# Weights converted in PSUM, squares mostly on GpSimd, raw weights in tiles of their own, half of batch 1's k^T q ahead of the FFN

## The chip, the cores and the metric

The kernel runs on one core of one Trainium2 chip. Its metric is the time of one execution on the device in microseconds (us), the median of several. Five engines work from instruction streams of their own: TensorE (PE), VectorE (DVE), ScalarE (ACT), GpSimd (POOL) and SyncE (SP), which here issues every DMA.

## The reference

Channel attention is followed by a feed-forward layer with a rational activation. B = 4, N = 6080, C = 256, d_ff = 2048. q, k, v are fp32, the two weight matrices fp64.

```python
qn = q / (norm(q, axis=1) + 1e-6);  kn = k / (norm(k, axis=1) + 1e-6)
a = softmax(kn.transpose(0, 2, 1) @ qn / tau)         # [B, 256, 256]
x = (v @ a).reshape(B * N, 256)
h = x @ w_in                                          # [24320, 2048]
g = (a0 + a1 h + a2 h^2 + a3 h^3) / (1 + |b0||h| + |b1| h^2 + 1e-6)
out = g @ w_out
```

## The kernel before

Each batch has 12 groups of 512 rows (the last has 448), 48 groups in all. The work is written as steps, each with an engine, an estimated cost, a key (a due time), the buffers it reads and writes, and a mark for steps that use the ports shared by VectorE and GpSimd. `Planner.order` plays these steps through before the kernel is built: on every engine it takes the ready step with the lowest key whose buffers are free, and writes down the order. On the chip each engine runs its steps in exactly that order. `SLOTS` says how many buffers a tag has; for the tags of the `fifo` list they are given out strictly in the order of the keys of the steps that open them.

**Attention (`Attn`).** A batch is read in 24 halves of a group, k and q of 256 rows, 512 KB (two DMAs). For a half ScalarE squares both (`ACT`, into an `sq` buffer), and the squares are added to one running sum: for batch 0 by VectorE, for the others by GpSimd. TensorE adds the products k^T q: batch 0 in one PSUM slot `hx` over all 24 halves, the other batches per pair of halves in an `hx` slot, which VectorE adds to `sacc` in SBUF. `softmax` then folds the sum, makes the norms, scales the scores into an `sq` buffer (`sn`), takes exponentials into a second one (`ex`), transposes, and `fuse` multiplies the attention into w_in for eight column blocks p (`w` buffers, split into a high and a low part).

**Weights (`piece`).** The fp64 weights come as pairs of 32-bit words, in 16 pieces of 512 KB: eight of w_in, eight of w_out. For each, ScalarE takes one absolute value and VectorE six operations of 512 elements make an fp32 piece. The first four pieces (`early`) use the tags `d`, `uu`, `r`; the other twelve have the raw words in `kq`, and work in `cv` and `cv2`. All of this is in SBUF.

**Main loop.** For each of the 48 groups `values` transposes v and splits it. `pair` does two blocks of 128 columns of the hidden layer, eight pairs a group, 384 in all: 12 matmuls into an `hx` slot, some twelve elementwise operations on ScalarE, VectorE and GpSimd, and 8 products with w_out (16 records) into the PSUM slot `acc`; `finish` copies `acc` out. PSUM holds three `hx` slots and one `acc`, each of two banks. Pairs p in `FACTORED` (p = 1 and 7, from the second group on) get the denominator from a VectorE product in place of GpSimd's addition. `LAG` holds the due times of a pair's steps behind its first, `TIME` those of all else; `T0` = 48.71 is the key of the first pair. Batch 1's attention has keys from T0 on, so it runs beside the first groups.

Of the kernel before, what the change touches and what calls it, by code (L numbers as in the profile page):

```python
# [18 lines left out]


LAG = {
    "first": 2.89, "prod": 5.51, "abs": -9.36, "line": 9.43, "second": 4.09, "sum": -23.2, "slope": 4.25,
    "num1": 24.9, "num2": 15.62, "root": 7.62, "one": 1.56, "square": 8.72, "again": 13.14, "quot": 7.51,
    "last": 10.86, "out": 34.22,
}
TIME = {
    "pair": 3.65, "start": 48.71, "load": 1.9, "softmax": 55.08, "in": 7.55, "late_in": 4.93, "out0": 1.91,
    "out": 6.15, "attn0_0": -0.12, "attn_0": 0.95, "attn0": 3.78, "attn": 2.7, "attn1": 91.81, "value": 3.3,
    "fuse": 1.89, "finish": 9.56,
}  # L30


# [35 lines left out]
class Planner:  # L68
# [1 line left out]

    HOP = {"PE": 0.25, "ACT": 0.07, "DVE": 0.07, "POOL": 0.07, "SP": 2.0}

    def __init__(self, slots, fifo, banks):
        self.slots, self.fifo, self.banks = slots, fifo, banks
# [34 lines left out]
    def order(self):  # L111
# [10 lines left out]
        events, out, now = [], [], 0.0  # L122
        port = {"DVE": 0.0, "POOL": 0.0}
        for s in self.steps:
            if not s.need:
# [13 lines left out]
        while left:  # L139
            for e in ready:  # L140
                while busy[e] <= now and ready[e]:
                    skipped, pick = [], None
                    while ready[e]:
                        entry = heapq.heappop(ready[e])
                        if fits(entry[2]):
                            pick = entry[2]
                            break
                        skipped.append(entry)
                    for entry in skipped:
                        heapq.heappush(ready[e], entry)  # L150
                    if pick is None:
                        break
                    for b in pick.new:
                        b.slot = free[b.tag].pop(0)
                        if b.tag in queue:
                            queue[b.tag].pop()
                    out.append((now, pick))
                    left -= 1
                    busy[e] = now + pick.cost
                    if pick.port:  # L160
                        other = "POOL" if e == "DVE" else "DVE"
                        busy[e] = max(now, port[other]) + pick.cost
                        port[e] = busy[e]
                    for b in pick.banks:
                        b.owner, b.until = e, busy[e] + self.HOP[e]
                    heapq.heappush(events, (busy[e], 0, pick.n, pick))
                    heapq.heappush(events, (busy[e] + self.HOP[e], 1, pick.n, pick))
            if not left:
                break
            assert events, [(e, h[0][0], [b.tag for b in h[0][2].new], dict(free)) for e, h in ready.items() if h]  # L170
            now = events[0][0]
            while events and events[0][0] <= now:
                _, what, _, s = heapq.heappop(events)
                for t in s.after:
# [14 lines left out]
def tile_channel_attention_rational_ffn(  # L189
# [15 lines left out]
    P = 128  # L205
# [9 lines left out]
    while n0 < N:  # L215
# [5 lines left out]
    TG = B * NG  # L221


    FACTORED = (1, 7)

    pe = InOrder(tc, nc.tensor)
    dve = InOrder(tc, nc.vector)
# [2 lines left out]
    sp = InOrder(tc, nc.sync)  # L230

    SLOTS = {"hx": 3, "acc": 1, "d": 4, "uu": 4, "r": 3, "g": 4, "w": 10, "kq": 4, "sq": 2, "ssq": 1,
             "vst": 1, "vhi": 2, "vlo": 2, "orow": 2, "sacc": 1, "eT": 1, "cv": 2, "cv2": 1, "n2": 1,
             "s0": 1, "y": 1, "e": 1, "sm": 1}
    plan = Planner(SLOTS, ("d", "uu", "r", "g", "w", "kq", "sq", "cv", "cv2", "vst", "vhi", "vlo", "orow"), ("hx", "acc"))
# [59 lines left out]
    def piece(side, m, at, c):  # L295
# [5 lines left out]
            src = w_in[j * P : (j + 1) * P, cols]  # L301
        else:
            src = w_out.rearrange("(f p) e -> p f e", p=P)[:, 2 * m : 2 * m + 2, :]
        early = side == "in" and m < 4
        raw = buf("d" if early else "kq", [P, 2 * PIECE], U32, "raw")
        work = buf("uu" if early else "cv", [P, 2, PIECE], F32, "work")
        unit = buf("r" if early else "cv2", [P, PIECE], U32, "unit")

        def keep():
            return work[:, 0]  # L310

        def top(kind=U32):
            return work[:, 1].bitcast(kind)

        def load():
# [4 lines left out]
        def lo():  # L320
            return raw.tile.rearrange("p (n w) -> p n w", w=2)[:, :, 0]
# [9 lines left out]
            dve.scalar_tensor_tensor(top(), hi(), 0xC0000000, top(), op0=ALU.bitwise_and, op1=ALU.bitwise_or)  # L331

        def power():
            dve.tensor_scalar(unit.tile, top(), 0xFF800000, None, op0=ALU.bitwise_and)

        def low_word():

            rest = unit.tile.bitcast(F32)
            dve.scalar_tensor_tensor(rest, lo(), 2.0**-52, rest, op0=ALU.mult, op1=ALU.mult)

        def together():
            rest = unit.tile.bitcast(F32)
            dve.tensor_tensor(rest, rest, top(F32), op=ALU.add)

        def cut_off():


            dve.scalar_tensor_tensor(
                dst, keep(), 1.125 * 2.0**-15, unit.tile.bitcast(F32), op0=ALU.is_ge, op1=ALU.mult
            )  # L350

        if side == "in":
            dst, ok = w_in_sb[:, j, cols], w_in_ok[part, j]
        else:
            dst, ok = w_out_sb[:, 2 * m : 2 * m + 2].rearrange("p f e -> p (f e)"), w_out_ok[m]
        step("SP", 1.5, at, load, (), [raw])
        step("ACT", 0.67, c, lambda: act.activation(keep(), hi().bitcast(F32), AF.Abs), [raw], [work])
        step("DVE", 0.45, c, low_bits, [raw, work], [work], True)
        step("DVE", 0.7, c + 0.1, high_bits, [raw, work], [work], True)
        step("DVE", 0.45, c + 0.2, power, [work], [unit], True)  # L360
        step("DVE", 0.7, c + 0.3, low_word, [raw, unit], [unit], True)
        step("DVE", 0.7, c + 0.4, together, [work, unit], [unit], True)
        step("DVE", 0.7, c + 0.5, cut_off, [work, unit], [ok], True)


    class Attn:
# [3 lines left out]
        def __init__(self, b, begin, pace, end, gate=()):  # L370
            self.b, self.gate, self.kq = b, gate, [None, None]
            self.ssq = None
            first = b == 0
            sps = buf("hx", [P, 2, GT], F32, "sps") if first else None
            self.sacc = None if first else buf("sacc", [P, 512], F32)
            for i in range(2 * NG):
                both = begin + (i if first else i + 1 - i % 2) * pace
                self.half(i, begin + i * pace, both, sps)
            self.scores = sps if first else self.sacc
            self.softmax(end)  # L380

        def half(self, i, at, both, sps):
# [2 lines left out]
            g, half = divmod(i, 2)  # L385
            base, pn = groups[g]
            first = self.b == 0
            kq = buf("kq" if not first or i % 6 < 3 else "r", [P, T // 2, 2, C], F32, "kq")

            def load():  # L390
                for j, src in ((0, k), (1, q)):
                    rows = src[self.b, base : base + pn * T].rearrange("(p t) c -> p t c", t=T)
                    sp.dma_start(kq[:pn, :, j, :], rows[:, half * T // 2 : (half + 1) * T // 2, :])

            step("SP", 1.4, at - (0 if first else 2 * II), load, self.gate, [kq])

            self.kq[half] = kq
            if first:
                fn = lambda: self.products(sps, [kq], pn, i == 0, i == 2 * NG - 1)
                step("PE", 1.75, both, fn, [kq, sps] if i else [kq], [sps])  # L400
            elif half == 1:
                pair, slot = list(self.kq), buf("hx", [P, 2, GT], F32, "sps")
                step("PE", 3.5, both, lambda: self.products(slot, pair, pn, True, True), pair, [slot])
                if g == 0:
# [9 lines left out]
            else:  # L414
                sq, total = buf("sq", [P, 2 * 2 * C], F32), self.ssq
                step("ACT", 1.05, at, lambda: act.activation(sq[:pn], src[1](), AF.Square), [kq], [sq])
                e = dve if first else pool
                fn = lambda: e.tensor_tensor(total[:pn], sq[:pn], total[:pn], op=ALU.add)
                step(*(("DVE", 1.2) if first else ("POOL", 2.38)), at + 2, fn, [sq, total], [total], True)
# [306 lines left out]
```

## Time and profile before

| | |
|---|---|
| median of 3 runs | 2726.62 us (2725.29 to 2728.51) |
| profiled execution | 2728.66 us |
| its span, first to last instruction | 2726.8 us |
| mean granted TensorE clock | 0.988 of full |
| HBM read, written | 83.10 MB, 24.90 MB |

The profile shows one execution. Its times are counted from the span's start. The busy time of an engine is the union of its instructions; a wait is put down to whoever ended it. Nearly all instructions carry one line (L43, the helper that records them), so groups are told apart by tile. In a timeline "x8" is eight records merged; fp32 matmuls leave two records each.

### The profile page before, as it was taken

Reading aid. Unit: us, or ns where it says so; the run is one execution under the profiler, and the core shown is the slowest. Engines: PE = TensorE matmul, PEld = TensorE weight load, DVE = VectorE, ACT = ScalarE, POOL = GpSimd, SP = SyncE. Lnnn points to the kernel's source line nnn. Section 1 sums busy time; section 2 is a strip of 40 time slices with the busy share of each in tenths; the row PEclk is TensorE's granted clock in tenths of the full one; section 3 lists DMA queues with packets and bytes.
Section 4 is the critical chain, followed back from the end, with each engine's and each line's share of the span. In section 5 each row is a group of like instructions: output and inputs, shape, how many; then the busy total and the mean of one; then the engine's idle time right before and its main releaser. Section 6 shows DMA issues by size and latency. Waiting matters only on the chain.

```text
span 2726.8 us, 32436 instructions
## 1 busy us (share of the span) xinstructions
PE 2662.3 (98%) x12200; PEld 2275.8 (83%) x12200; DVE 2195.9 (81%) x1962; ACT 2182.7 (80%) x2227; POOL 2171.5 (80%) x1134
## 2 busy tenths in 40 slices
PE   7689999999999999999999999999999999999999
PEld 6478888888888888888888888888888888888887
DVE  6887888888887777777897877877888888888886
ACT  4467888888888888877887888887887888888886
POOL 0389887888868898987876989888885887887885
PEclk8799999999999999999999999999999999999999
DMA  8222100000001111110000111110000000000000
GB/s 260 93 86 86 60 24 16 24 24 15 32 15 47 47 47 47 47 45 31 31 16 31 34 52 54 47 45 16 31 16 16 17 29 16 24 24 16 31 8 15
DMA packets 69325, 110.10 MB, mean 40 GB/s; under 512 B 5296, under 2 KB 53936, under 8 KB 69168
## 3 DMA queue, kind: packets, MB, share of 16 engines
q1 hardware_dynamic: 69168, 108.03, 12.2%
q8 instruction: 96, 1.57, 0.2%
q14 instruction: 61, 0.50, 0.1%
HBM read 83.10 MB, written 24.90 MB: 40 GB/s over the span
## 4 chain that ended last, share of the span: by engine, by line
PE 86%; DVE 4%; POOL 4%; ACT 2%; DMA 2%; issue 2%; SPq 0%; POOLq 0%; ACTq 0%; DVEq 0%
PE acc L43 44%; PE hx L43 42%; POOL d L43 3%; ACT r L43 1%; DVE hx L43 1%; DMA r<-in_q_dram 1%; POOL ssq L43 1%; ACT uu L43 1%; DVE cv L43 1%; DMA kq<-in_q_dram 0%; DVE g L43 0%; DVE uu L43 0%; DVE sq L43 0%; DVE y L43 0%; DVE sm L43 0%
## 5 line engine op out<-in xcount | busy, mean ns | idle before, releaser
L43 PE MATMUL acc<-w_out_sb,g 128*128 128x256 f32 (+1 forms) x6144 | 1379.7, 379 | 0.0
L43 PEld LDWEIGHTS acc<-w_out_sb,g 128*128 128x128 f32 (+1 forms) x6144 | 1156.1, 189 | 169.0
L43 PE MATMUL hx<-vhi,w 128*128 128x512 f32 (+1 forms) x3072 | 1034.0, 404 | 7.1 <-DVE g L43 3.3
L43 POOL TENSOR_TENSOR d<-d,r 128x1024 f32<-128x1024 f32 (+1 forms) x384 | 905.0, 2364 | 129.4 <-ACT r L43 124.2
L43 POOL TENSOR_TENSOR d<-d,uu 128x1024 f32<-128x1024 f32 (+1 forms) x290 | 685.0, 2362 | 27.2 <-ACT uu L43 4.2
L43 PEld LDWEIGHTS hx<-vhi,w 128*128 128x128 f32 x3072 | 578.6, 188 | 126.3 <-DVE g L43 5.9
L43 DVE TENSOR_TENSOR uu<-uu,hx 128x1024 f32<-128x1024 f32 (+1 forms) x384 | 463.1, 1206 | 256.9 <-ACT uu L43 255.3
L43 PE MATMUL hx<-vlo,w 128*128 128x512 f32 (+1 forms) x1536 | 596.9, 389 | 0.0
L43 DVE SCALAR_TENSOR_TENSOR hx<-hx,coef,r 128x1024 f32<-128x1024 f32 (+1 forms) x384 | 490.1, 1277 | 67.0 <-ACT r L43 59.8
L43 DVE SCALAR_TENSOR_TENSOR g<-d,hx 128x1024 f32<-128x1024 f32 (+1 forms) x384 | 463.1, 1207 | 80.5 <-POOL d L43 57.0
L43 ACT ACTIVATE r<-d 128x1024 f32<-128x1024 f32 (+1 forms) x384 | 405.5, 1056 | 127.3 <-POOL d L43 124.3
L43 DVE SCALAR_TENSOR_TENSOR hx<-uu,coef,hx 128x1024 f32<-128x1024 f32 (+1 forms) x384 | 488.9, 1273 | 6.1
L43 ACT ACTIVATE uu<-hx,coef 128x1024 f32<-128x1024 f32 (+1 forms) x384 | 461.8, 1203 | 0.0
L43 ACT ACTIVATE uu<-hx,babs 128x1024 f32<-128x1024 f32 (+1 forms) x384 | 424.8, 1106 | 33.7 <-PE hx L43 33.7
L43 ACT ACTIVATE d<-hx 128x1024 f32<-128x1024 f32 (+1 forms) x290 | 294.3, 1015 | 163.1 <-PE hx L43 160.9
L43 ACT ACTIVATE r<-r 128x1024 f32<-128x1024 f32 (+1 forms) x384 | 405.5, 1056 | 6.9
L43 POOL TENSOR_SCALAR d<-d,babs 128x1024 f32<-128x1024 f32 (+1 forms) x290 | 325.6, 1123 | 86.4 <-ACT d L43 85.7
L43 PEld LDWEIGHTS hx<-vlo,w 128*128 128x128 f32 x1536 | 289.8, 189 | 55.2
L43 POOL TENSOR_TENSOR ssq<-sq,ssq 128x1024 f32<-128x1024 f32 (+1 forms) x69 | 165.1, 2392 | 120.6 <-ACT sq L43 119.8
L43 POOL TENSOR_SCALAR d<-d,ones 128x1024 f32<-128x1024 f32 (+1 forms) x94 | 105.0, 1117 | 174.5 <-ACT r L43 170.8
L43 PE MATMUL hx<-kq 128*128 128x256 f32 (+1 forms) x672 | 159.4, 392 | 17.4 <-issue 8.4
L43 PEld LDWEIGHTS hx<-kq 128*128 128x128 f32 (+1 forms) x672 | 131.7, 197 | 38.8 <-DMA kq<-in_k_dram 16.4
(73 smaller groups left out, 1004.0 us busy)
## 6 DMA issues: line engine op xcount, KB each, us to landing
vst<-in_v_dram SPq DMA_DIRECT2D x44, 512.0 KB, 3.5
out_dram<-orow SPq DMA_DIRECT2D x44, 512.0 KB, 2.6
kq<-in_k_dram SPq DMA_DIRECT2D x78, 256.0 KB, 3.6
kq<-in_q_dram SPq DMA_DIRECT2D x78, 256.0 KB, 3.9
kq<-in_moe_w_out_dram SPq DMA_DIRECT2D x8, 512.0 KB, 3.7
r<-in_k_dram SPq DMA_DIRECT2D x10, 256.0 KB, 5.7
r<-in_q_dram SPq DMA_DIRECT2D x10, 256.0 KB, 6.0
d<-in_moe_w_in_dram SPq DMA_DIRECT2D x4, 512.0 KB, 6.5
```

The source lines that it names most:

```text
L43: ins = op(*args, **kwargs)
```

## The change

The diff, with the new numbers of `LAG`, `TIME` and `HOP` cut to those that steps below use:

```diff
 LAG = {
-    "first": 2.89, "second": 4.09, "slope": 4.25, "last": 10.86, "out": 34.22, ...
+    "first": 2.42, "second": 3.75, "slope": 5.71, "last": 10.3, "out": 23.21, ...
 TIME = {
-    "pair": 3.65, "start": 48.71, "load": 1.9, "softmax": 55.08, "in": 7.55, "late_in": 4.93, "out0": 1.91,
-    "out": 6.15, ...
+    "pair": 3.57, "start": 48.71, "load": 1.9, "softmax": 48.77, "in": 5, "late_in": 3.83, "out0": 2.3,
+    "out": 5.39, ... "front": 45.32, "front_pace": 2.4,
-    HOP = {..., "SP": 2.0}
+    HOP = {..., "SP": 3.5}
+        busy["SP"] = 3.0        # in the planner: SP is taken until 3.0
-    FACTORED = (1, 7)
+    FACTORED = (1, 3, 6)
+    EARLY = [("in", m) for m in range(8)] + [("out", m) for m in range(4)]
+    FRONT = 12
-  SLOTS: "cv": 2;  fifo: (..., "orow")
+  SLOTS: "cv": 1;  fifo: (..., "orow", "acc")
 def piece(side, m, at, c):
-        early = side == "in" and m < 4
-        raw = buf("d" if early else "kq", [P, 2 * PIECE], U32, "raw")
-        work = buf("uu" if early else "cv", [P, 2, PIECE], F32, "work")
-        unit = buf("r" if early else "cv2", [P, PIECE], U32, "unit")
+        early = (side, m) in EARLY
+        raw = buf("d" if early else "g", [P, 2 * PIECE], U32, "raw")
+        kept = buf("uu" if early else "cv", [P, 2, PIECE], F32, "kept")
+        work = buf(("acc" if side == "in" and m < 4 else "hx") if early else "cv2", [P, 2, PIECE], F32, "work")
+        port = not early
...
-        step("SP", 1.5, at, load, (), [raw])
-        step("ACT", 0.67, c, ...Abs, [raw], [work])
-        step("DVE", 0.45, c, low_bits, [raw, work], [work], True)
-        step("DVE", 0.7, c + 0.1, high_bits, [raw, work], [work], True)
-        step("DVE", 0.45, c + 0.2, power, [work], [unit], True)
-        step("DVE", 0.7, c + 0.3, low_word, [raw, unit], [unit], True)
-        step("DVE", 0.7, c + 0.4, together, [work, unit], [unit], True)
-        step("DVE", 0.7, c + 0.5, cut_off, [work, unit], [ok], True)
+        step("SP", 1.65, at, load, (), [raw])
+        step("ACT", 0.67, c, ...Abs, [raw], [kept])
+        one, two = (0.62, 0.7) if early else (0.45, 0.7)
+        step("DVE", one, c, low_bits, [raw], [work], port)
+        step("DVE", two, c + 0.1, high_bits, [raw, work], [work], port)
+        step("DVE", one, c + 0.2, power, [work], [work], port)
+        step("DVE", two, c + 0.3, low_word, [raw, work, kept], [kept], port)
+        step("DVE", two, c + 0.4, together, [work, kept], [work], port)
+        step("DVE", two, c + 0.5, cut_off, [work, kept], [ok], port)
 class Attn:
+            self.front = FRONT if b == 1 else 0
+            if self.front:
+                sps = buf("acc", [P, 2, GT], F32, "fronts")
             for i in range(2 * NG):
+                if i < self.front:
+                    at = both = TIME["front"] + i * TIME["front_pace"]
...
-            step("SP", 1.4, at - (0 if first else 2 * II), load, self.gate, [kq])
+            step("SP", 1.6, at - (0 if first else 3 if i < self.front else 2 * II), load, self.gate, [kq])
-            if first:
-                fn = lambda: self.products(sps, [kq], pn, i == 0, i == 2 * NG - 1)
+            if first or i < self.front:
+                fn = lambda: self.products(sps, [kq], pn, i == 0, i == (self.front or 2 * NG) - 1)
                 step("PE", 1.75, both, fn, [kq, sps] if i else [kq], [sps])
+                if i == self.front - 1:
+                    fn = lambda: dve.tensor_copy(self.sacc.tile, sps[:, 0, :])
+                    step("DVE", 0.66, both + 1, fn, [sps], [self.sacc])
...
-                e = dve if first else pool
+                own = first and i % 4 == 3
+                e = dve if own else pool
...
-    for m in range(4):
-        c = 18.0 + TIME["in"] * m
-        piece("in", m, c - 6.0, c)
-    late = [("in", m, TIME["late_in"] * (m - 4)) for m in range(4, 8)]
-    late += [("out", m, TIME["out0"] + TIME["out"] * m) for m in range(NFP)]
+    for n, (side, m) in enumerate(EARLY):
+        c = 8.0 + TIME["in"] * n
+        piece(side, m, min(c, 36.0 + 0.1 * n) - 6.0 if side == "in" else c - 6.0, c)
+    late = [("out", m, TIME["out0"] + TIME["out"] * m) for m in range(NFP) if ("out", m) not in EARLY]
```

Twelve pieces instead of four are early: raw words in `d`, the kept half in `uu`, and the working halves in PSUM, in `acc` for the first four and in `hx` for the other eight. The four late pieces (w_out 4 to 7) have raw words in `g`. Of batch 0's 23 additions of squares VectorE does every fourth half's (i = 3, 7, ..., 23) and GpSimd 17. Halves 0 to 11 of batch 1 have keys from 45.32 on, 2.4 apart; their products go into one `acc` slot and are copied to `sacc` once, after the twelfth.

## Rows read from the trace of the kernel before

**Rows 1.** The page's part 1: busy us (share of the span) x instructions.
```profile
PE 2662.3 (98%) x12200; PEld 2275.8 (83%) x12200; DVE 2195.9 (81%) x1962; ACT 2182.7 (80%) x2227; POOL 2171.5 (80%) x1134
```

**Rows 2.** Stretches: length; busy PE, PEld, DVE, ACT, POOL; clock, DMA share, GB/s.
```profile
2.60:64.80 62.20, 46.12 (x188) 38.98 (x189) 42.32 (x51) 30.02 (x32) 0.00 (x0) 0.90 0.93 285
66.00:99.00 33.00, 14.88 (x38) 10.32 (x36) 31.87 (x55) 9.63 (x15) 2.34 (x1) 0.60 0.36 112
99.00:123.20 24.20, 15.98 (x61) 12.89 (x61) 17.46 (x26) 16.83 (x21) 11.95 (x6) 0.78 0.25 87
123.20:210.00 86.80, 79.00 (x334) 66.15 (x335) 73.81 (x68) 56.72 (x64) 71.19 (x35) 0.94 0.23 73
210.00:310.00 100.00, 99.84 (x460) 85.10 (x459) 74.32 (x65) 82.00 (x82) 98.27 (x49) 1.00 0.30 94
310.00:740.00 430.00, 430.00 (x1990) 369.49 (x1989) 360.30 (x301) 361.10 (x360) 355.95 (x189) 1.00 0.06 21
```

**Rows 3.** TensorE's timeline, 98 to 194: start, us, operation [idle before <-releaser].
```profile
98.96 7.77 PE L43 MATMUL hx<-w_in_sb,eT 128*128 128x256 f32 x24 [0.68 <-ACT eT L43]
...
123.15 1.97 PE L43 MATMUL hx<-ident,vst 128*128 128x128 f32 x8 [8.22 <-DVE g L43]
...
190.54 3.62 PE L43 MATMUL hx<-kq 128*128 128x256 f32 x16
193.99 3.62 PE L43 MATMUL acc<-w_out_sb,g 128*128 128x256 f32 x16
```

**Rows 4.** VectorE's timeline, 65 to 123.
```profile
65.90 1.23 DVE L43 TENSOR_TENSOR orow<-sq,orow 112x1024 f32<-112x1024 f32 x1 [0.29 <-ACT sq L43]
...
68.37 0.42 DVE L43 TENSOR_SCALAR cv<-kq 128x512 uint32<-128x512 uint32 x1
...
72.07 0.42 DVE L43 TENSOR_SCALAR cv<-kq 128x512 uint32<-128x512 uint32 x1
...
75.84 0.69 DVE L43 TENSOR_TENSOR orow<-orow 128x512 f32<-128x512 f32 x1
...
84.63 0.13 DVE L43 TENSOR_SCALAR n<-y,rtau 128x2 f32<-128x2 f32 x1
...
91.23 0.87 DVE L43 SCALAR_TENSOR_TENSOR sq<-hx,n,y 128x256 f32<-128x256 f32 x2
...
92.86 2.01 DVE L43 TENSOR_SCALAR sm<-sm 128x2 f32<-128x2 f32 x1
...
121.89 1.21 DVE L43 SCALAR_TENSOR_TENSOR g<-d,hx 128x1024 f32<-128x1024 f32 x1
```

**Rows 5.** ScalarE's timeline at 91.
```profile
91.36 1.06 ACT L43 ACTIVATE sq<-kq 128x1024 f32<-128x1024 f32 x1 [1.55 <-DMA kq<-in_q_dram]
```

**Rows 6.** GpSimd's timeline, its first two operations of this work.
```profile
92.50 2.34 POOL L43 TENSOR_TENSOR ssq<-sq,ssq 128x1024 f32<-128x1024 f32 x1 [91.05 <-ACT sq L43]
110.66 1.64 POOL L43 TENSOR_SCALAR d<-d,babs 128x1024 f32<-128x1024 f32 x1 [15.81 <-ACT d L43]
```

**Rows 7.** Groups by form: shapes xcount | busy us, mean ns | idle before.
```profile
L43 POOL TENSOR_TENSOR ssq<-sq,ssq 128x1024 f32<-128x1024 f32 x63 | 150.8, 2394 | 120.6 <-ACT sq L43 119.8
...
L43 DVE SCALAR_TENSOR_TENSOR w<-hx,sm,w 128x256 fp32r<-128x256 f32 x64 | 27.9, 478 | 17.1 <-ACT w L43 17.1
...
L43 DVE TENSOR_TENSOR sacc<-hx,sacc 128x512 f32<-128x512 f32 x33 | 22.6, 685 | 10.4 <-PE hx L43 10.3
...
L43 DVE TENSOR_SCALAR uu<-d 128x512 uint32<-128x512 uint32 x4 | 1.7, 423 | 0.8 <-DMA d<-in_moe_w_in_dram 0.8
...
L43 DVE TENSOR_SCALAR n<-hx 128x258 f32<-128x258 f32 x4 | 1.7, 420 | 0.0
```

**Rows 8.** The chain of waits at the end: start, us, what.
```profile
2700.97 20.73 PE acc L43 x96
```

More of the change, by code (lines that the diff above doesn't have):

```diff
@@ L21 @@
 LAG = {
-    "first": 2.89, "prod": 5.51, "abs": -9.36, "line": 9.43, "second": 4.09, "sum": -23.2, "slope": 4.25,
-    "num1": 24.9, "num2": 15.62, "root": 7.62, "one": 1.56, "square": 8.72, "again": 13.14, "quot": 7.51,
-    "last": 10.86, "out": 34.22,
+    "first": 2.42, "prod": 2.04, "abs": -4.64, "line": 9.56, "second": 3.75, "sum": -23.6, "slope": 5.71,
+    "num1": 23.17, "num2": 21.53, "root": 8.83, "one": -1.7, "square": -3.23, "again": 5.54, "quot": 8.31,
+    "last": 10.3, "out": 23.21,
 }
 TIME = {
-    "pair": 3.65, "start": 48.71, "load": 1.9, "softmax": 55.08, "in": 7.55, "late_in": 4.93, "out0": 1.91,
-    "out": 6.15, "attn0_0": -0.12, "attn_0": 0.95, "attn0": 3.78, "attn": 2.7, "attn1": 91.81, "value": 3.3,
-    "fuse": 1.89, "finish": 9.56,
+    "pair": 3.57, "start": 48.71, "load": 1.9, "softmax": 48.77, "in": 5, "late_in": 3.83, "out0": 2.3,
+    "out": 5.39, "attn0_0": -0.02, "attn_0": 0.98, "attn0": 3.82, "attn": 2.42, "attn1": 91.81, "value": 3.3,
+    "fuse": 1.77, "finish": 10.12, "front": 45.32, "front_pace": 2.4,
 }
@@ L68 @@
 class Planner:
-    HOP = {"PE": 0.25, "ACT": 0.07, "DVE": 0.07, "POOL": 0.07, "SP": 2.0}
+    HOP = {"PE": 0.25, "ACT": 0.07, "DVE": 0.07, "POOL": 0.07, "SP": 3.5}
     def __init__(self, slots, fifo, banks):
@@ L121, in order @@
         busy = {e: 0.0 for e in self.HOP}
-        events, out, now = [], [], 0.0
+        busy["SP"] = 3.0
+        events, out, now = [(3.0, 2, 0, None)], [], 0.0
         port = {"DVE": 0.0, "POOL": 0.0}
@@ L173, in order @@
                 _, what, _, s = heapq.heappop(events)
+                if what == 2:
+                    continue
                 for t in s.after:
@@ L232, in tile_channel_attention_rational_ffn @@
     SLOTS = {"hx": 3, "acc": 1, "d": 4, "uu": 4, "r": 3, "g": 4, "w": 10, "kq": 4, "sq": 2, "ssq": 1,
-             "vst": 1, "vhi": 2, "vlo": 2, "orow": 2, "sacc": 1, "eT": 1, "cv": 2, "cv2": 1, "n2": 1,
+             "vst": 1, "vhi": 2, "vlo": 2, "orow": 2, "sacc": 1, "eT": 1, "cv": 1, "cv2": 1, "n2": 1,
              "s0": 1, "y": 1, "e": 1, "sm": 1}
-    plan = Planner(SLOTS, ("d", "uu", "r", "g", "w", "kq", "sq", "cv", "cv2", "vst", "vhi", "vlo", "orow"), ("hx", "acc"))
+    plan = Planner(SLOTS, ("d", "uu", "r", "g", "w", "kq", "sq", "cv", "cv2", "vst", "vhi", "vlo", "orow", "acc"), ("hx", "acc"))
     const = ctx.enter_context(tc.tile_pool(name="const", bufs=1))
@@ L303, in piece, with unit @@
             src = w_out.rearrange("(f p) e -> p f e", p=P)[:, 2 * m : 2 * m + 2, :]
-        early = side == "in" and m < 4
-        raw = buf("d" if early else "kq", [P, 2 * PIECE], U32, "raw")
-        work = buf("uu" if early else "cv", [P, 2, PIECE], F32, "work")
-        unit = buf("r" if early else "cv2", [P, PIECE], U32, "unit")
+        early = (side, m) in EARLY
[3 more added lines that the diff above has]
+        port = not early
         def keep():
-            return work[:, 0]
+            return kept[:, 0]
         def top(kind=U32):
+            return work[:, 0].bitcast(kind)
+        def unit(kind=U32):
             return work[:, 1].bitcast(kind)
@@ L333, in power @@
         def power():
-            dve.tensor_scalar(unit.tile, top(), 0xFF800000, None, op0=ALU.bitwise_and)
+            dve.tensor_scalar(unit(), top(), 0xFF800000, None, op0=ALU.bitwise_and)
         def low_word():
-            rest = unit.tile.bitcast(F32)
-            dve.scalar_tensor_tensor(rest, lo(), 2.0**-52, rest, op0=ALU.mult, op1=ALU.mult)
+            dve.scalar_tensor_tensor(kept[:, 1], lo(), 2.0**-52, unit(F32), op0=ALU.mult, op1=ALU.mult)
         def together():
-            rest = unit.tile.bitcast(F32)
-            dve.tensor_tensor(rest, rest, top(F32), op=ALU.add)
+            dve.tensor_tensor(unit(F32), kept[:, 1], top(F32), op=ALU.add)
         def cut_off():
             dve.scalar_tensor_tensor(
-                dst, keep(), 1.125 * 2.0**-15, unit.tile.bitcast(F32), op0=ALU.is_ge, op1=ALU.mult
+                dst, keep(), 1.125 * 2.0**-15, unit(F32), op0=ALU.is_ge, op1=ALU.mult
             )
@@ L355, in piece @@
             dst, ok = w_out_sb[:, 2 * m : 2 * m + 2].rearrange("p f e -> p (f e)"), w_out_ok[m]
-        step("SP", 1.5, at, load, (), [raw])
-        step("ACT", 0.67, c, lambda: act.activation(keep(), hi().bitcast(F32), AF.Abs), [raw], [work])
-        step("DVE", 0.45, c, low_bits, [raw, work], [work], True)
-        step("DVE", 0.7, c + 0.1, high_bits, [raw, work], [work], True)
-        step("DVE", 0.45, c + 0.2, power, [work], [unit], True)
-        step("DVE", 0.7, c + 0.3, low_word, [raw, unit], [unit], True)
-        step("DVE", 0.7, c + 0.4, together, [work, unit], [unit], True)
-        step("DVE", 0.7, c + 0.5, cut_off, [work, unit], [ok], True)
+        step("SP", 1.65, at, load, (), [raw])
+        step("ACT", 0.67, c, lambda: act.activation(keep(), hi().bitcast(F32), AF.Abs), [raw], [kept])
+        one, two = (0.62, 0.7) if early else (0.45, 0.7)
[5 more added lines that the diff above has]
+        step("DVE", two, c + 0.5, cut_off, [work, kept], [ok], port)
     class Attn:
@@ L375, in __init__ @@
             self.sacc = None if first else buf("sacc", [P, 512], F32)
+            self.front = FRONT if b == 1 else 0
+            if self.front:
+                sps = buf("acc", [P, 2, GT], F32, "fronts")
             for i in range(2 * NG):
-                both = begin + (i if first else i + 1 - i % 2) * pace
-                self.half(i, begin + i * pace, both, sps)
+                if i < self.front:
+                    at = both = TIME["front"] + i * TIME["front_pace"]
+                else:
+                    at, both = begin + i * pace, begin + (i if first else i + 1 - i % 2) * pace
+                self.half(i, at, both, sps)
             self.scores = sps if first else self.sacc
@@ L387, in half @@
             first = self.b == 0
-            kq = buf("kq" if not first or i % 6 < 3 else "r", [P, T // 2, 2, C], F32, "kq")
+            home = "r" if first and i % 6 >= 3 else "kq"
+            kq = buf(home, [P, T // 2, 2, C], F32, "kq")
             def load():
@@ L403, in half @@
                 step("PE", 3.5, both, lambda: self.products(slot, pair, pn, True, True), pair, [slot])
-                if g == 0:
+                if i == 1:
                     fn = lambda: dve.tensor_copy(self.sacc.tile, slot[:, 0, :])
@@ L416, in half @@
                 step("ACT", 1.05, at, lambda: act.activation(sq[:pn], src[1](), AF.Square), [kq], [sq])
-                e = dve if first else pool
+                own = first and i % 4 == 3
+                e = dve if own else pool
                 fn = lambda: e.tensor_tensor(total[:pn], sq[:pn], total[:pn], op=ALU.add)
-                step(*(("DVE", 1.2) if first else ("POOL", 2.38)), at + 2, fn, [sq, total], [total], True)
+                step(*(("DVE", 1.2) if own else ("POOL", 2.38)), at + 2, fn, [sq, total], [total], True)
         def products(self, slot, halves, pn, first, last):
```

## The prediction

> **What bounds the kernel now.** I read the shares of busy time first: TensorE is busy 98% of the span, VectorE 81%, GpSimd 80% [rows 1]. Then the stretches. From 310 to 740 us TensorE is busy 430.00 of 430 us at full clock [rows 2]: nothing but less TensorE work shortens that stretch. What is left lies ahead of it. The reader is to see three stretches in [rows 2]: up to 64.8 the DMA engines are 0.93 busy at 285 GB/s (batch 0's k and q come in); from 66 to 99 TensorE is busy 14.88 of 33 us and VectorE 31.87; from 99 to 210 TensorE is idle 8.2 + 7.8 = 16.0 us and runs at granted clocks of 0.78 and 0.94. From 210 to 310 TensorE is full again, with GpSimd at 98.27 of 100.
>
> Third, the order of VectorE's work between 66 and 99 [rows 4]. The last square of batch 0 is added at 65.90 and done at 67.1. The fold that opens the softmax starts only at 75.84; the two weight pieces in front of it take 3.70 us each (68.37 to 72.07 is one). The norms' scale is there at 84.76 (84.63 + 0.13), yet the score scaling starts at 91.23: 6.5 us of weight conversion lie between. Its reason is in the buffer order: the scaled scores take an "sq" buffer, these are given out in the order of their keys, and the square of batch 1's second half comes before them. That square ran at 91.36, straight after a wait for its DMA [rows 5], and its load had to wait for a "kq" buffer, which the raw weights occupied. So the first fuse matmul runs at 98.96 [rows 3].
>
> **The change part by part.** Signs: minus is time saved.
>
> *Start of the first fuse.* Squares: 17 of 23 additions of batch 0 go from VectorE (1.23 us, [rows 4]) to GpSimd (2.39 us, [rows 7]), which does nothing before 92.50 [rows 6]. The chain through the one sum takes 17 x 2.39 + 6 x 1.23 = 48 us and starts at about 10, beside loads that end after 60, so the loads decide. In the new order 35 loads of 512 KB stand up to batch 0's last half: 24 halves, 8 pieces of w_in, one of w_out, one v, one front half. The 285 GB/s of [rows 2] give 1.84 us for each at a busy share of 0.93, 1.71 at full share. The last lands at 2.6 + 35 x 1.71 = 62.5 to 67; I take 64. A square (1.06) and VectorE's own addition of half 23 (1.23) follow: fold at 66.5. Bounds 60 and 70. Against 75.84 this is -9.3.
>
> *The 6.5 us stall.* Raw weights no longer sit in "kq", and front half 1 has load key 44.72, right behind half 23 (43.7) and four late w_out loads (43.8 to 44.1). It lands some five or six loads later, near 74, before the scores are due (66.5 + 84.76 - 75.84 = 75.4). I count -6.5; bounds -6.5 and 0. Filler instructions of conversions, each one instruction deep, and PSUM buffers that pieces 8 and 9 hold while the norms want one, give back about 1. First fuse at 98.96 - 9.3 - 6.5 + 0.8 = 84. Term: **-15**, bounds -22 to -6.
>
> *Conversion in PSUM.* No row shows a 512-wide tensor_scalar on PSUM. Below: 0.42 as in SBUF; above and taken: 0.685, the addition of the same width with a PSUM operand [rows 7]. The three scalar_tensor_tensor lie between that 0.685 and twice the 256-wide one (0.478), 0.96; I take 0.8. A piece costs 3 x 0.685 + 3 x 0.8 = 4.5 us against 3.70 (bounds 3.70 and 4.9). Until 66 VectorE then has 8 or 9 pieces and 6 additions: 9 x 4.5 + 7.4 = 48 of some 57 us. The loads cover it; without that cover 9 x 0.8 = 7 us would be late. Count 0.
> That a 258-wide operation from PSUM takes 0.42, as long as the 512-wide one in SBUF [rows 7], shows the loss. The Trainium skill, "VectorE: DVE Perf Modes", section "Why PSUM operands drop a tier", says the same of any PSUM operand, that it ends the two-port mode; by it the piece is dearer as above and the sum does not move. It speaks against the change only where VectorE is the bound, which is no longer so before 66.
>
> *Products moved to the front.* Sixteen products of a pair of halves take 193.99 - 190.54 = 3.45 us of TensorE [rows 3]. Twelve halves are six pairs, 20.7 us; one pair already lay ahead of the first fuse before, so 5 x 3.45 = 17.25 us leave the full stretch. But only halves 0 to 5 find buffers early: squares from half 2 on need an "sq" buffer after the softmax's two, so "kq" (four buffers) stays full until the exponentials are done, near 80. Then GpSimd adds halves 2 to 5 in 4 x 2.39 = 9.6 us, buffers come free, and half 11 lands near 96. Its products end near 99. So six halves, 6 x 1.73 = 10.4 us, fall into the ramp, where TensorE sat idle for 8.22 us before 123.15, waiting for g [rows 3]. They fill that. Net -17.25 + 10.4 - 8.2 = **-15**; bounds -17.25 (all hidden) and -6.9 (none).
> The sum's bank "acc" must be free when the first w_out product is due: g of pair 0 runs at 121.89 to 123.1, 24 us after the first fuse [rows 3, 4], so at 108 now. The last front product and its copy (0.685) end at about 100: hidden, with 8 us of slack.
>
> *Later weights.* Raw w_out pieces 2 and 3 take "d" buffers by key (52 and 57), behind pair 0's (48.71 + 2.42 = 51.13). So they load only once the pairs run, and are converted in one of three "hx" buffers, which the pairs need. Each holds one for about 6 us, 12 buffer-us over 3 buffers: 4 us, a part of it beside the latency of the first pairs. **+3**, bounds 0 and +8. The four last pieces stay in SBUF and meet GpSimd as now; raw in "g" delays nothing as long as one is converted before 108.
>
> *Third factored pair in eight.* It takes one GpSimd addition from one pair in eight and gives VectorE one product. In the full stretch both lie beside TensorE: 0. In 123 to 210 GpSimd loses 12 additions of squares (29 us) and these; idle there was 7.8 us [rows 2]. **-1**, bounds -4 and 0. New keys for the order: 0, bounds -2 and +8. At the end TensorE works off w_out products for 20.73 us without a gap [rows 8], so the last pairs' other engines are covered.
>
> *Sum:* -15 - 15 + 3 - 1 = -28 us. The profiled execution took 2728.66 us for a span of 2726.8, 1.9 around it; the median of the three is 2726.62, 2.0 lower. I carry the saving over to the median: **2698.6 us**.
>
> **The rivals.** *A, the port.* GpSimd adds front squares while the softmax runs, and VectorE's operations with two SBUF inputs wait for it. For it: with GpSimd's addition at 92.50 running, a two-element operation of VectorE took 2.01 us at 92.86 [rows 4, 6]. Against: until the exponentials only front half 1 has an "sq" buffer, one addition. If the additions came without a break, eight operations (fold, five of the norms, two small ones) would each wait some 1.9 us: 15 us, and the time is 2698.6 + 15 = 2713.6.
> The Trainium skill, "SBUF — State Buffer", section "Who interferes with whom", calls this pair of ports an exclusive lock held for a whole instruction, taken by operations with two SBUF inputs. By that rule A would happen wherever the additions are dense; the 2.01 us agrees. It also says that one PSUM operand frees a conversion of it: the fuse's scaling, with one, took 0.478 on average in 64 cases [rows 7].
>
> *C, the ramp is not filled.* Front loads come late, TensorE waits for them in order, and the hx buffers cost their upper bound: -15 - 6.9 + 8 = -14, 2712.7. For it: TensorE's order is fixed. Against: slack of 8 us.
>
> *A and C together:* -14 + 15 = +1, 2727.6, no change.
>
> *B, the bank is held.* "acc" is one buffer; if front half 11 is late, no w_out product can run, four g and three hx buffers fill and TensorE stands. Each us beyond 108 costs one. It decides for slower beyond 108 + 28 = 136. That comes if all ten additions from half 2 on alternate with the pairs' work on GpSimd, 8 us a turn: 80 + 83 = 163, 55 late, 2753.6. For it: four kq, two sq and one ssq buffer in a row. Against: GpSimd's first pair work came 11.7 us after the first fuse (110.66, [rows 6]), at 96 now, and only four additions stand before half 11's load.
>
> *More is won:* loads at the faster bound and all products hidden, -28 - 6 - 2 = -36 or more, 2690 and below.
>
> **How the numbers follow.** Forecast 0.62, A 0.14, C 0.08, more 0.06, A with C 0.04, B 0.06. Some 0.2% (5.5 us) is what a measurement of this kernel tells from no change. Faster: 0.62 + 0.14 + 0.08 + 0.06 = 0.90; same 0.04; slower 0.06. The range for 8 in 10 takes in the forecast with its bounds, most of A and C, and a part of "more": 2682 to 2715.
>
> **What would show it.** Right: first fuse at 80 to 88; no conversion of 6 us between scale and scores; GpSimd additions of 2.4 us from 10 on; conversions of 4.2 to 4.9 us a piece that keep their length beside GpSimd; 12 halves' products into acc ending before the first g; TensorE's 99-to-210 idle time of 16 us down to some 10; full from about 200 on. Wrong: softmax operations of 2 us or more (A); TensorE idle behind front loads (C) or in front of the first w_out product with g long done (B); TensorE under 99% in the full stretch, which would make the third factored pair a cost.

## The result, and the profile after

The changed kernel takes 2693.03 us (median of 4, 2692.60 to 2694.12) against 2725.95 us of before: 32.9 us less, ratio 0.9879, 95% interval 0.9862 to 0.9896. The forecast was 2698.6 us. The profiled execution took 2692.95 us for a span of 2691.2; spans differ by 35.6 us, because before's profiled execution was 2.7 us above its median. What follows is reckoned in spans.

Part 1 of the page after answers to [rows 1]:

```profile
PE 2650.2 (98%) x12200; PEld 2269.1 (84%) x12200; DVE 2247.8 (84%) x1987; ACT 2196.4 (82%) x2227; POOL 2108.5 (78%) x1104
```

GpSimd lost 63 us of busy time (2171.5 to 2108.5), VectorE gained 52. The stretches, in the columns of [rows 2]:

```profile
2.60:64.80 62.20, 51.17 (x213) 42.24 (x214) 47.02 (x65) 34.62 (x38) 40.25 (x17) 0.97 1.05 339
66.00:99.00 33.00, 30.16 (x128) 25.39 (x129) 31.03 (x40) 22.34 (x31) 21.65 (x10) 0.91 0.61 189
99.00:210.00 111.00, 102.23 (x454) 86.06 (x453) 101.72 (x98) 88.85 (x96) 99.25 (x49) 0.97 0.18 57
...
310.00:740.00 430.00, 427.20 (x1982) 367.18 (x1981) 373.85 (x327) 363.96 (x370) 333.12 (x177) 1.00 0.06 20
```

Loads came at 339 GB/s where they had come at 285, and from 66 to 99 TensorE was busy 30.16 us instead of 14.88. From 99 to 210 it was idle 8.8 us instead of 16.0, at a granted clock of 0.97; before, its two parts had 0.78 and 0.94 [rows 2]. From 310 to 740 it now lost 2.8 us; before none.

VectorE's timeline after (start, us, operation), beside [rows 4]:

```profile
10.22 0.69 DVE L43 TENSOR_SCALAR acc<-d 128x512 uint32<-128x512 uint32 x1 [5.05 <-DMA d<-in_moe_w_in_dram]
...
14.66 0.69 DVE L43 TENSOR_SCALAR acc<-d 128x512 uint32<-128x512 uint32 x1
...
18.04 0.69 DVE L43 SCALAR_TENSOR_TENSOR uu<-d,acc 128x512 f32<-128x512 uint32 x1
...
61.95 1.23 DVE L43 TENSOR_TENSOR orow<-sq,orow 112x1024 f32<-112x1024 f32 x1 [1.12 <-ACT sq L43]
63.21 0.69 DVE L43 TENSOR_TENSOR orow<-orow 128x512 f32<-128x512 f32 x1
...
68.39 2.53 DVE L43 SCALAR_TENSOR_TENSOR e<-e,s 128x258 f32<-128x258 f32 x1
...
73.59 0.13 DVE L43 TENSOR_SCALAR n<-y,rtau 128x2 f32<-128x2 f32 x1
73.75 0.88 DVE L43 SCALAR_TENSOR_TENSOR sq<-hx,n,y 128x256 f32<-128x256 f32 x2
...
106.03 1.21 DVE L43 SCALAR_TENSOR_TENSOR g<-d,hx 128x1024 f32<-128x1024 f32 x1
...
113.72 0.68 DVE L43 COPY sacc<-acc 128x512 f32<-128x512 f32 x1
```

A piece's first two starts, 10.22 and 14.66, are 4.44 us apart, all six operations at 0.69 or 0.70; the one at 18.04 kept its 0.69 beside the GpSimd additions from 17.25 on, shown below. The fold ran at 63.21, straight behind the last addition, and the score scaling at 73.75 straight behind the scale at 73.59. One operation of the norms took 2.53 us, at 68.39: GpSimd's addition of front half 1 had begun at 68.29.

```profile
17.25 7.27 POOL L43 TENSOR_TENSOR orow<-sq,orow 128x1024 f32<-128x1024 f32 x3 [1.84 <-ACT sq L43]
...
68.29 2.35 POOL L43 TENSOR_TENSOR ssq<-sq,ssq 128x1024 f32<-128x1024 f32 x1 [7.89 <-ACT sq L43]
79.24 10.72 POOL L43 TENSOR_TENSOR ssq<-sq,ssq 128x1024 f32<-128x1024 f32 x4 [8.61 <-ACT sq L43]
```

TensorE after, beside [rows 3]:

```profile
58.65 1.97 PE L43 MATMUL acc<-kq 128*128 128x256 f32 x8 [1.91 <-DMA kq<-in_q_dram]
...
67.19 11.12 PE L43 MATMUL acc<-kq 128*128 128x256 f32 x40 [2.13 <-DMA kq<-in_q_dram]
...
79.64 3.72 PE L43 MATMUL hx<-w_in_sb,eT 128*128 128x256 f32 x16 [0.89 <-ACT eT L43]
83.20 1.89 PE L43 MATMUL acc<-kq 128*128 128x256 f32 x8
...
91.42 3.61 PE L43 MATMUL acc<-kq 128*128 128x256 f32 x16
...
96.59 3.62 PE L43 MATMUL acc<-kq 128*128 128x256 f32 x16
...
110.51 1.89 PE L43 MATMUL acc<-kq 128*128 128x256 f32 x8
...
116.28 1.89 PE L43 MATMUL acc<-w_out_sb,g 128*128 128x256 f32 x8
```

The first fuse is at 79.64 (before 98.96). Of the front halves' 96 records 8 + 40 lie ahead of it and 8 + 16 + 16 + 8 behind, the last at 110.51; VectorE copied the sum at 113.72, though the first g had run at 106.03, and the first w_out product came at 116.28.

From the first fuse to the copy of the last output it was 2622.8 us (2721.7 less 98.96) and is 2606.4 (2686.05 less 79.64). So the 35.6 us are 19.3 ahead of the first fuse and 16.4 behind it. Of the 16.4, 32 records less (16 front records before, 48 now) at 3.45/16 = 0.216 us are 6.9. The idle time from 99 to 210 gave 7.2. The clock and the stretch from 79.64 to 99 are in the rest, which I did not divide. The later softmaxes take some back, a wait of TensorE that before did not have, against 6.4 us of other waits before (engine, line waited for: us in total, times, longest):

```profile
PE hx L43 <- DVE sm L43: 8.4, 3, 2.8
```

Counted in TensorE's records the whole gain shows in one place. Up to 310 us, before and after (columns of [rows 2]):

```profile
0.00:310.00 310.00, 257.01 (x1079) 214.38 (x1080) 240.70 (x263) 197.54 (x214) 184.59 (x96) 0.90 0.41 127
0.00:310.00 310.00, 283.81 (x1255) 239.37 (x1256) 262.09 (x270) 227.52 (x245) 248.66 (x126) 0.97 0.41 130
```

These are 176 records more, 38 us at 0.216; from 310 to 2680 they are 8 fewer (10920 against 10928), -1.7 us. Together that makes 36.3 us; the spans differ by 35.6.

### The profile page after: what moved, and what is told of

It reads as the page before. It is cut to its first block, busy times and chain, and to the rows that moved or that the text cites. A ratio compares the mean times of both kernels' runs of the same rounds, so it can differ in the third digit from the quotient of the medians.

```text
span 2691.2 us, 32473 instructions
## 1 busy us (share of the span) xinstructions
PE 2650.2 (98%) x12200; PEld 2269.1 (84%) x12200; DVE 2247.8 (84%) x1987; ACT 2196.4 (82%) x2227; POOL 2108.5 (78%) x1104
## 4 chain that ended last, share of the span: by engine, by line
PE 90%; DVE 3%; POOL 1%; ACT 1%; issue 0%; DVEq 0%; POOLq 0%
PE acc L43 47%; PE hx L43 44%; DVE hx L43 1%; POOL d L43 1%; DVE g L43 1%; DVE sq L43 0%; ACT r L43 0%; DVE cv L43 0%; DVE uu L43 0%; DVE y L43 0%; DVE n L43 0%; DVE vlo L43 0%; DVE e L43 0%; ACT d L43 0%; DVE sm L43 0%
## 5 line engine op out<-in xcount | busy, mean ns | idle before, releaser
L43 PE MATMUL hx<-vhi,w 128*128 128x512 f32 (+1 forms) x3072 | 1018.3, 402 | 10.2 <-DVE g L43 5.3
L43 POOL TENSOR_TENSOR d<-d,uu 128x1024 f32<-128x1024 f32 (+1 forms) x243 | 574.4, 2364 | 20.3
L43 ACT ACTIVATE d<-hx 128x1024 f32<-128x1024 f32 (+1 forms) x243 | 247.4, 1018 | 223.8 <-PE hx L43 223.5
L43 POOL TENSOR_SCALAR d<-d,babs 128x1024 f32<-128x1024 f32 (+1 forms) x243 | 273.4, 1125 | 163.1 <-ACT d L43 162.3
L43 POOL TENSOR_SCALAR d<-d,ones 128x1024 f32<-128x1024 f32 (+1 forms) x141 | 157.8, 1119 | 140.7 <-ACT r L43 140.6
L43 ACT ACTIVATE d<-d 128x1024 f32<-128x1024 f32 (+1 forms) x141 | 146.5, 1039 | 57.3 <-DVE d L43 57.3
L43 DVE SCALAR_TENSOR_TENSOR d<-uu,babs,hx 128x1024 f32<-128x1024 f32 (+1 forms) x141 | 178.2, 1264 | 12.9 <-ACT uu L43 12.9
```

Of the source, the lines that this page charges most:

```text
L43: ins = op(*args, **kwargs)
```

## The experiments

Each stands against the changed kernel's 2693.0 us, and has its own ratio to before, which was measured beside it (medians of 2726.2 to 2727.0 us).

**Front halves.**

```diff
-    FRONT = 12
+    FRONT = 0          # and in a second run: 6
```

> The changed kernel (2693.0) with FRONT = 0: batch 1's halves all go through hx and sacc again, at their old keys. Theory (the front halves are worth TensorE work taken out of the full stretch): in the changed kernel 6 of the 12 front halves run before the first fuse and 6 in the ramp. Without them 6 x 1.73 = 10.4 us come back into the full stretch, and up to 8 us of ramp idle are no longer filled; the first fuse stays near 79.6. 2703 to 2712. Rival (they only move, since TensorE has to do them anyway and GpSimd does their squares in either place): 2689 to 2697.

> The changed kernel with FRONT = 6: the acc slot is free some 25 us earlier, and halves 6 to 11 of batch 1 go through hx in the full stretch. In the changed kernel the copy of the front sum ran at 113.7, after the first g at 106.0, and the first w_out product at 116.3. Theory (the front halves fill TensorE's ramp and the late bank costs little): 6 x 1.73 = 10.4 us come back, less the 2 to 5 us that the bank held up; 2697 to 2704. Rival (the held bank costs as much as the halves win): 2690 to 2695.

FRONT = 0: 2710.7 us (0.9939, 0.9924 to 0.9954), 17.6 more, in the theory's range. FRONT = 6: 2710.4 us (0.9941, 0.9928 to 0.9955), 17.4 more, above the ranges of its theory and of its rival. The first fuse stayed, at 79.53 and 79.42, and the first g even came earlier, at 100.36 and 101.57 instead of 106.03. Without front halves:

```profile
66.00:99.00 33.00, 21.21 (x85) 16.44 (x84) 28.83 (x43) 22.22 (x31) 20.44 (x9) 0.94 0.44 144
99.00:210.00 111.00, 102.60 (x444) 86.00 (x444) 97.01 (x90) 78.41 (x86) 90.19 (x44) 0.94 0.20 62
```

That is 85 + 444 = 529 records of TensorE from 66 to 210 where the changed kernel had 582; with 6 it was 518. Some 53 to 64 records of 0.216 us, 11 to 14 us, were missing there and had to be done in the full stretch; up to 310 us it was 1190 and 1187 records instead of 1255, 14 to 15 us. Six halves alone won nothing: it is the other six, in the ramp, that use its idle time. The bank that they held up to 113.7 cost less than they brought.

**Where the weights work, and who adds the squares.**

```diff
 # first and third run
-  work = buf(("acc" if side == "in" and m < 4 else "hx") if early else "cv2", ...);  port = not early
-  one, two = (0.62, 0.7) if early else (0.45, 0.7)
+  work = buf("cv2", ...);  port = True
+  one, two = 0.45, 0.7
 # second and third run
-  own = first and i % 4 == 3
+  own = first
```

> The changed kernel with the working halves of all sixteen pieces in the one SBUF buffer cv2 instead of PSUM, so each operation on them has its operands in SBUF. Theory (PSUM matters because it keeps VectorE off the ports that GpSimd's additions use): GpSimd is busy 40 of 62 us with additions before the fold; each of the 54 operations of the nine pieces in front of the fold then can wait up to 1.7 us behind one, and the additions wait too. The first fuse comes 15 to 35 us later, at 95 to 115: 2708 to 2728. Rival (it matters little where they work, the loads set the pace; an operation in SBUF is even shorter, 0.42 against 0.69): first fuse within 3 us, 2690 to 2697.

> The changed kernel with all 23 of batch 0's additions on VectorE. Theory (VectorE was the bound in front of the fold, so its relief counts): VectorE is busy some 47 of the first 63 us now; 17 x 1.23 = 21 us more do not fit. Fold and first fuse come 5 to 12 us later, 2698 to 2706. Rival (the loads set the pace; GpSimd's chain of additions, 8.6 us for four halves, is itself the slower one): first fuse at 79.6 or up to 3 us earlier, 2689 to 2695.

> All pieces work in the one SBUF buffer, as in the run with SBUF work (2758.0), and VectorE does all 23 additions of batch 0, as in the run with squares on VectorE (2708.3). Port theory (the 65 us of the first run came from VectorE and GpSimd waiting for each other): without GpSimd's additions a piece takes 3.7 us again, the fold comes at 70 to 78, and the time is 2703 to 2718. Rival (the single working buffer, with pieces one behind the other, made the 65 us): 2740 or more.

SBUF work: 2758.0 us (1.0114, 1.0099 to 1.0129), 65 more, nearly twice the first theory's upper end. Operations that need 0.43 and 0.69 took the length of a GpSimd addition, three of them beside three additions:

```profile
30.29 7.68 POOL L43 TENSOR_TENSOR orow<-sq,orow 128x1024 f32<-128x1024 f32 x3 [5.01 <-DVE orow L43]
...
30.52 2.74 DVE L43 SCALAR_TENSOR_TENSOR cv<-d,cv 128x512 uint32<-128x512 uint32 x1
33.29 2.46 DVE L43 TENSOR_SCALAR cv<-cv 128x512 uint32<-128x512 uint32 x1
35.79 2.74 DVE L43 SCALAR_TENSOR_TENSOR uu<-d,cv 128x512 f32<-128x512 uint32 x1
```

The fold came at 79.72, the first fuse at 99.25, as the first theory had it. But the rest of the loss lay behind that: TensorE stood for 32 us until the first g was there.

```profile
159.92 3.58 PE L43 MATMUL hx<-w_in_sb,eT 128*128 128x256 f32 x8 [32.03 <-DVE g L43]
```

Squares on VectorE: 2708.3 us (0.9931, 0.9914 to 0.9947), 15.3 more, a little beyond the theory. The fold came 12.4 us late, the first fuse at 91.04:

```profile
75.58 0.68 DVE L43 TENSOR_TENSOR orow<-orow 128x512 f32<-128x512 f32 x1
```

Both: 2746.8 us (1.0076, 1.0060 to 1.0091). The port theory was right about the fold (72.22) and wrong about the time; the time was the rival's. TensorE's timeline and VectorE's show why:

```profile
85.48 5.45 PE L43 MATMUL hx<-w_in_sb,eT 128*128 128x256 f32 x24 [1.01 <-ACT eT L43]
...
144.13 3.78 PE L43 MATMUL hx<-w_in_sb,eT 128*128 128x256 f32 x8 [32.92 <-DVE g L43]
```

```profile
116.60 2.45 DVE L43 TENSOR_SCALAR cv<-cv 128x512 uint32<-128x512 uint32 x1
119.18 2.62 DVE L43 SCALAR_TENSOR_TENSOR uu<-d,cv 128x512 f32<-128x512 uint32 x1
121.84 2.71 DVE L43 TENSOR_TENSOR cv<-uu,cv 128x512 f32<-128x512 f32 x1
...
142.87 1.21 DVE L43 SCALAR_TENSOR_TENSOR g<-d,hx 128x1024 f32<-128x1024 f32 x1
```

The first fuse was there at 85.48, but VectorE still had w_out pieces to make, in SBUF, beside GpSimd's work for the first pairs and batch 1: up to 2.77 us an operation, up to the first g at 142.87. From 92.63 to there VectorE never stood, and 19 operations of pieces took 44.0 us where 0.42 and 0.69 each make 11.5. The 32.5 us between are as long as TensorE's wait of 32.92. So it was the ports, but in the ramp; a buffer that pieces waited for would have left VectorE idle. What the single buffer does to the order was not told apart.

**The keys alone.** The kernel before with the new LAG, TIME (without "in"), costs of SP and FACTORED:

> The kernel before with nothing but the new numbers: LAG, TIME, the planner's costs and hop of SP, FACTORED (1, 3, 6). Buffers, engines and the place of batch 1's halves as before. Theory (the gain is in the parts, the keys only fit them): within 8 us of before, 2718 to 2734. Rival (the new keys do most of it, by a better order): below 2710.

2729.6 us (1.0010, 1.0001 to 1.0019): no gain, as expected. Yet its profile was the surprise of the study. The first fuse ran at 74.58, earlier than in the changed kernel, without any of the new buffers. Then TensorE stood for 22.69 us:

```profile
74.58 8.50 PE L43 MATMUL hx<-w_in_sb,eT 128*128 128x256 f32 x24 [0.68 <-ACT eT L43]
...
118.38 3.64 PE L43 MATMUL hx<-w_in_sb,eT 128*128 128x256 f32 x8 [22.69 <-DVE g L43]
```

```profile
93.21 2.78 DVE L43 TENSOR_TENSOR cv<-cv,cv 128x512 f32<-128x512 f32 x1
96.02 2.73 DVE L43 SCALAR_TENSOR_TENSOR w_in_sb<-cv,cv 128x512 f32<-128x512 f32 x1
...
99.12 2.72 DVE L43 SCALAR_TENSOR_TENSOR cv<-kq,cv 128x512 uint32<-128x512 uint32 x1
...
117.11 1.22 DVE L43 SCALAR_TENSOR_TENSOR g<-d,hx 128x1024 f32<-128x1024 f32 x1
```

The new order had put the weights behind the softmax; VectorE made them between 70 and 113, six operations at 2.46 to 2.78 us beside GpSimd, and the first g came at 117.11 (before 121.89, changed 106.03). TensorE had done 1089 records up to 310 us, before 1079: an early first fuse alone is worth nothing.

**Raw weights in kq.**

```diff
-        raw = buf("d" if early else "g", ...)
+        raw = buf("d" if early else "kq", ...)
```

> The changed kernel with the raw words of the four late pieces back in kq. First theory (the prediction's: raw words in kq kept batch 1's half from its buffer, and the score scaling stood 6.5 us): the stall between scale and scores comes back, 5 us or more, and front halves come later; 2698 to 2708. Second theory (formed on the run with only the new keys, which has raw words in kq and no stall: the first fuse was there at 74.6): keys already put the weights behind, so the stall does not return; first fuse within 3 us of 79.6, 2690 to 2698.

2699.6 us (0.9901, 0.9886 to 0.9916), 6.5 more. The time falls into the first theory's range and just above the end of the second's; the mechanism is neither's:

```profile
73.47 0.88 DVE L43 SCALAR_TENSOR_TENSOR sq<-hx,n,y 128x256 f32<-128x256 f32 x2
...
127.15 0.68 DVE L43 COPY sacc<-acc 128x512 f32<-128x512 f32 x1
```

The scaling did not wait (73.47), the first fuse was 2.3 us late, and the copy of the front sum came at 127.15 instead of 113.72, though the first g was earlier (102.99). The raw words took the front halves' buffers: front half 1 was loaded from 66.24 on instead of 57.74, and TensorE had done 1231 records up to 310 us instead of 1255, 5 us.

**Factored pairs.**

```diff
-    FACTORED = (1, 3, 6)
+    FACTORED = (1, 7)      # in a second run with the old LAG too
```

> The changed kernel with FACTORED = (1, 7). Theory (TensorE is the bound in the full stretch, GpSimd has room at either setting there): 2691 to 2696. Rival 1 (the third factored pair is what lets GpSimd carry batch 1's squares between 99 and 310): slower, 2698 to 2706. Rival 2 (it costs, since TensorE lost 2.8 us of 430 in the full stretch that it did not lose before): 2687 to 2690.

> The changed kernel with the old LAG (due times inside a pair) and FACTORED = (1, 7). FACTORED alone cost 40.6 us. First theory (the due times inside a pair belong to their FACTORED; either set alone fills the full stretch): the old set brings the full stretch back to 430 of 430 us busy and the front stays; 2689 to 2700. Second theory (with the new front and the other new numbers two factored pairs in eight no longer keep up): 2715 to 2740.

2733.7 us (1.0026, 1.0017 to 1.0036), 40.6 more: rival 1's direction at three times its upper end, and in the full stretch, which it did not name. The full stretch and TensorE's wait in it:

```profile
310.00:740.00 430.00, 419.42 (x1929) 358.24 (x1928) 359.97 (x308) 359.16 (x362) 349.07 (x184) 1.00 0.06 20
```

```profile
PE hx L43 <- DVE g L43: 28.9, 16, 3.7
```

From 310 to 740, 800 to 1400, 1400 to 2000 and 2000 to 2680 TensorE did 10460 records, the changed kernel 10650: 190 x 0.216 = 41 us. With the old LAG as well it was 2723.7 us (0.9991, 0.9982 to 1.0001) and 10529 records; the first theory fell, and the time lies in the second's range. The kernel before fills that stretch with (1, 7) and its own numbers (10663 records). So two factored pairs fall behind with the rest of the change. Which part of it does that (TIME, SP's costs, the order of "acc", the buffers) stays open.

**Pace of batch 0, and three tries for more.**

```diff
-  own = first and i % 4 == 3
+  own = first and i % 3 == 2
```

> The changed kernel with VectorE adding every third half of batch 0 (8 of 23) instead of every fourth (6). Theory (the chain of additions sets the pace in front of the fold: ScalarE waited 14 times for a GpSimd addition, 15.4 us in all, and GpSimd never stood more than 2.5 us): the chain gets 15 x 2.42 + 8 x 1.4 = 47.5 us against 49.7, so the fold comes about 2 us earlier; VectorE has 15 us of room. 2689 to 2692. Rival (loads set the pace, as the prediction had it): fold within 0.5 us of 63.2, 2692 to 2695.

2692.4 us (0.9878, 0.9864 to 0.9891), the fold at 63.19: the rival's. Loads set the pace, though narrowly. The last square of batch 0 waited for its load here, and in the changed kernel for a buffer that a GpSimd addition freed:

```profile
60.77 1.06 ACT L43 ACTIVATE sq<-r 112x1024 f32<-112x1024 f32 x1 [0.99 <-DMA r<-in_q_dram]
...
60.79 1.06 ACT L43 ACTIVATE sq<-r 112x1024 f32<-112x1024 f32 x1 [1.14 <-POOL orow L43]
```

In the changed kernel the load and the chain of additions end within 0.3 us of each other, so a shorter chain alone wins nothing.

```diff
-  work = buf("acc" ... "hx" ... if early else "cv2", ...)
+  work = buf("acc" if side == "in" and m < 4 else "hx", ...)   # port = False, all costs 0.62 and 0.7, no "cv2"
-  "kq": 4
+  "kq": 5                                                     # second run only
```

> The changed kernel with the four late pieces in PSUM too (working halves in hx, kept half in cv, no cv2). In the changed kernel their operations of 0.43 to 0.69 us took up to 2.89 between 79 and 125, beside GpSimd. Theory (VectorE's waits for the ports are what is late in the ramp): some 12 us of VectorE's time come back, 5 to 8 of them on the path: 2685 to 2690. Rival (the three hx slots are what is short in the ramp, and the late pieces take one each for some 5 us): 2693 to 2702.

> As the run before, with a fifth kq buffer in the room that cv2 had. In the changed kernel the front halves' loads stood from 71 to 79 for want of a buffer, and the copy of the front sum came at 113.7, 6.5 us behind the first g. Theory (buffers hold the front sum, and through it the first w_out products): the copy comes 2 to 5 us earlier and 1 to 4 us are won over the run with all pieces in PSUM. Rival (GpSimd's additions hold it, not the buffers): within 1 us of that run.

2695.6 us (0.9889, 0.9874 to 0.9904) and 2695.65 us (0.9887, 0.9871 to 0.9904). VectorE's busy time from 99 to 210 fell from 101.72 to 89.39 us, and nothing was won:

```profile
99.00:210.00 111.00, 104.18 (x461) 87.67 (x461) 89.39 (x89) 90.66 (x99) 94.81 (x48) 0.97 0.17 53
```

The copy of the front sum came at 104.50 and 106.36, 7 to 9 us earlier, and that won nothing either. Both times are the rivals'; that the hx slots are what is short, as the first of them has it, no run shows. No run beat the changed kernel beyond the intervals.

## Why the prediction was right, point by point

**First fuse, -15.** Measured -19.3, inside the bounds, though 79.64 lies just ahead of the 80 to 88 named as a sign. The fold was at 63.2 (forecast 66.5), since the last of the 35 loads had landed by 60.8, 1.66 us a load; I had worked with 1.71 and then taken 64. That loads set the pace held (every third addition on VectorE changed nothing). But the step took one thing for granted: that what is won at the first fuse is won at the end. The keys alone won 24.4 us there and nothing at the end. What the end follows is how many records TensorE gets done before the full stretch: 1079 up to 310 us before, 1089 with the keys alone, 1186 with squares on VectorE, 1255 in the changed kernel. At 0.216 us each, with the few that differ behind 310, they account for the spans of these runs to within 1 us; neither the first fuse nor the first g does. So the -15 was right as a time, but that it reached the end hung on the conversion, priced at 0: with SBUF work and squares on VectorE the first fuse came at 85.48, near the forecast 84, and the time was 2746.8 us. In that the sum had luck. "The loads cover it [the conversion]" held for the 48 us that were put on VectorE, and has its limit: with 21 us more the fold was 12.4 us late and the time 15.3 us longer.

**The stall, -6.5.** It went, but not for the reason given. Raw words in kq with the new keys make no stall: in the kernel before (scale at 68.52, scaling at 68.68) as in the changed one, the keys had ended it. What the new tile is worth, 6.5 us, lies in the front halves. That it equals the forecast is chance.

**Conversion in PSUM, 0.** 4.44 us a piece against 4.5 forecast, in part by chance: the scalar_tensor_tensor took 0.69 and not 0.8, and the gaps between the six operations, which the sum left out, made up for it. The 0 was true of the change as made, and hid the largest dependence: in SBUF it would have cost 65 us. The two parts are one: with squares on GpSimd the conversion must be off the ports, and with squares on VectorE it still cost 38 us (2746.8 against 2708.3), beside GpSimd's work in the ramp. The row fits what the Trainium skill states ("SBUF — State Buffer", "Who interferes with whom"): an operation with two SBUF inputs contends with one of GpSimd's that reads SBUF, and the pair of ports that they share is an exclusive lock. The same scalar_tensor_tensor took 2.74 us with both inputs in SBUF and 0.69 with one in PSUM, beside the same additions. It fits "VectorE: DVE Perf Modes" ("Why PSUM operands drop a tier") as well, by which a PSUM operand ends the two-port mode: the same 512-wide tensor_scalar took 0.42 in SBUF [rows 7] and 0.69 on PSUM.

**Products to the front, -15.** The count was exact, 48 records ahead of the first fuse and 48 behind. The bank came free at 114.4 and not at 100, so the sign that these products end before the first g did not come: rival B's mechanism began, 7 us behind the first g, but TensorE had fuses and front products to do and the earlier copies of the last two runs won nothing. Without front halves 17.6 us are lost, against the 15 of the term.

**Later weights +3, relief of GpSimd -1, full stretch 0.** No run measured the +3 and the -1 apart. TensorE's idle time from 99 to 210 fell to 8.8 us, where "some 10" was forecast. The full stretch lost 2.8 us (10650 against 10663 records), of the kind the +8 bound was for. "Both lie beside TensorE: 0" is right as a sum and wrong as a reason: setting FACTORED back costs 40.6 us in exactly that stretch. There VectorE was busy 84% and GpSimd 81%, and TensorE still waited 28.9 us for VectorE's g. That the written-out order makes engines with room hold up the bound one is my reading; no run tested it apart.

**Rivals.** A happened once, for 2.1 us; the count of one addition that could get in the way was right. (The 2.01 us that spoke for A was a tensor_scalar with one tensor input; the case with two is the 2.53 at 68.39.) C did not come. B's cause did in part, without its price.

## What to carry to other kernels

Count what the bound engine has done by the time it is full, not when its main loop begins. An order can advance the first fuse by 24 us and win nothing, and a later first g can go with a faster kernel, where the bound engine has other work to fill the time. Cost a part that looks free by taking it out: conversion in PSUM and the factored pairs were worth 0 in the sum and 65 and 41 us when removed. In this kernel, whose order is written out from due times, the old FACTORED took 2733.7 us with the new LAG and 2723.7 with the old: numbers that were fitted together are to be changed together.

## What the runs showed of the hardware

Beside GpSimd's two-input additions, VectorE's operations with two SBUF inputs (and its tensor_scalar from SBUF to SBUF) took the length of an addition, 2.4 to 2.8 us instead of 0.42 to 0.69, one for one as long as additions follow each other; three additions in a row stretched from 7.27 to 7.68 us. Six operations of a piece with their working half in PSUM kept 0.69 beside the same additions. The loads reached 339 GB/s over 62 us, where 285 at a busy share of 0.93 had looked nearly full; with the new keys and the old buffers they stayed at 286.
